# A fused attention and FFN block: every piece placed by a list schedule, and the loads in order of use

## The chip, the cores and the metric

One core of a Trainium2 chip. The time is the device time of one execution in microseconds. The span is the time from the first to the last instruction of a profiled or timed run; it is some 2 us shorter than the time. Every run also gives the mean clock that TensorE was granted (1.0 is full speed). Runs are compared within the same rounds on the same chip, and only fast runs are; a run over 1.5% above the fastest of the same kernel counts as slow.

## What the kernel computes

A layer norm of x (2048 rows, 640 columns, bf16) feeds two branches, whose sum with x is the output:

```python
def _A_ref(x, wqkv, wo):            # 32 heads of 20; window of 8 keys, 2 apart
    qkv = (x @ wqkv).reshape(B, S, 3, H, Dh) ...
    idx = pos[:, None] - (jnp.arange(8) * 2)[None, :]
    logits = jnp.einsum("bhsd,bhswd->bhsw", q, kg) * Dh ** -0.5   # masked where idx < 0
    o = jnp.einsum("bhsw,bhswd->bhsd", softmax(logits), vg)
    return o.reshape(B, S, D) @ wo

def _B_ref(x, w1, b1, w2, b2):      # 640 -> 1536 -> 640
    return gelu(x @ w1 + b1) @ w2 + b2

xn = _layernorm(x)
return x + _A_ref(xn, A_wqkv, A_wo) + _B_ref(xn, B_w1, B_b1, B_w2, B_b2)
```

## The kernel before

The rows are worked on in four chunks of 512. For each chunk VectorE multiplies q with eight shifted copies of k, TensorE sums the products by head (the "logits"), softmax follows across TensorE, ScalarE and VectorE, TensorE expands the weights back over the head's columns (the "expansions"), and VectorE multiplies them with v. Projections, FFN and output blocks are dense matmuls. Products of TensorE pass through four accumulators (`psA`), the logits have a buffer of two banks, and an output block a pair of its own:

```python
    psA = ctx.enter_context(tc.tile_pool(name="psA", bufs=4, space=bass.MemoryType.PSUM))
    psL = ctx.enter_context(tc.tile_pool(name="psL", bufs=1, space=bass.MemoryType.PSUM))
    psO = ctx.enter_context(tc.tile_pool(name="psO", bufs=1, space=bass.MemoryType.PSUM))
    # ... (cut)
    load_x(0)                                  # four transfers on SyncE's queue
    for s in range(3):                         # q, k and v columns of wqkv
        nc.scalar.dma_start(wqkv_sb[:, :, s * D : (s + 1) * D], wqkv_v[:, :, s * D : (s + 1) * D])
    nc.sync.dma_start(b1_rt[0:FT, :], B_b1.rearrange("(t p) -> t p", p=P))
    load_x(1)
    nc.sync.dma_start(w1_sb[:], B_w1.rearrange("(t p) n -> p t n", p=P))
    # ... (cut: b2, w2, wo on SyncE's queue)
```

An output block is 18 pairs of matmuls and one eviction of two copies:

```python
    def outs(n):
        # ... (cut)
        for bl in range(BPC):
            # ... (cut: x is loaded again, VectorE adds b2 to it)
            lo = psO.tile([P, CH], F32, tag="lo", name="lo")
            hi = psO.tile([P, CH], F32, tag="hi", name="hi")
            srcs = [(hT[:, ft, cs], w2_sb[:, ft, :]) for ft in range(FT)]
            srcs += [(ident[:], xb2[:])]
            srcs += [(oT[:, t, cs], wo2[:, t, :]) for t in range(KT)]
            # ... (cut: for each of srcs one matmul into lo, one into hi)
            nc.scalar.copy(osb[:, 0:CH], lo[:])
            nc.scalar.copy(osb[:, CH:D], hi[:, 0 : D - CH])
            nc.scalar.dma_start(out_sd[b * P : (b + 1) * P, :], osb[:])
```

The framework's scheduler orders the pieces, by the order in which the program names them and by what is ready:

```python
    ln(0)
    qkv(0)
    ln(1)
    for n in range(NCH):
        attention(n)
        ffn1(n)
        if n + 1 < NCH:
            qkv(n + 1)
        # ... (cut: load and layer norm of chunk n + 2)
        if n > 0:
            outs(n - 1)
    outs(NCH - 1)
```

## Time and profile before

| | before |
|---|---|
| median (lowest to highest) | 278.5 us (274.83 to 278.62), 3 runs |
| profiled run | 276.86 us, span 275.1, mean TensorE clock 0.969 |
| TensorE busy | 233.7 us, 85% of the span |
| VectorE, ScalarE busy | 173.0 us, 125.0 us |

The prediction below shows the busy slices, the chain and the timelines. Here is only the list of TensorE's waits by matmul group (engine, output tile, line; after the arrow what ended the wait; then us in total, times, longest; lines are cut at the dots):

```profile
PE lo L336 <- ACT osb L341: 4.9, 8, 0.6
PE L L215 <- DVE prod L210: 3.6, 3, 2.1
PE xps L263 <- ACT ax L270: 2.7, 6, 0.7
...
PE pps L193 <- DMA wqkv_sb<-in_A_wqkv_dram: 1.7, 1, 1.7
```

A reader is to see two things. Most waits belong to steps of the attention, and most of that time lies in the first chunk, the only one in which TensorE has no other work to put beside them. And `lo` waits for its own eviction eight times. The list counts only what the profile sees as idle and models the end of a matmul late, so it understates: from start to start of the matmuls the eight waits are 0.78 each.

### The profile page before, as it was taken

How to read it: one execution, taken by the hardware profiler on the slowest of the kernel's cores; microseconds unless marked ns; L12 is line 12 of the kernel's file. 1: busy time of each engine (PE TensorE's matmuls, PEld its weight loads, DVE VectorE, ACT ScalarE, POOL GpSimd, SP SyncE). 2: the span in 40 equal slices, each digit the busy share in tenths (PEclk: the TensorE clock that was granted, in tenths of full speed). 3: DMA queues.
4: the chain of work that ended last, by engine and by line, in shares of the span. 5: the costliest groups of instructions: out<-in, count | busy, mean ns of one | idle time of the engine just before them, and what ended most of it. 6: DMA issues, size and time to landing. Idle time of an engine off the chain costs nothing.

```text
span 275.1 us, 3746 instructions
## 1 busy us (share of the span) xinstructions
PE 233.7 (85%) x1564; PEld 122.4 (44%) x1591; DVE 173.0 (63%) x191; ACT 125.0 (45%) x212; POOL 0.9 (0%) x8
## 2 busy tenths in 40 slices
PE   0049995379999989999999989999999899999895
PEld 0024553124455543445555634455556444455452
DVE  3850599869965956997592259994932399921000
ACT  0242562576655546765551458655313586211211
POOL 1000000000000000000000000000000000000000
PEclk9999998559999999999999999999999999999999
DMA  7999203000000000000011110000021100111010
GB/s 249 373 335 381 92 2 95 24 4 0 0 0 2 0 26 24 0 2 0 0 49 49 50 49 0 2 0 0 10 88 50 48 0 0 50 48 48 26 48 24
DMA packets 11416, 15.47 MB, mean 56 GB/s; under 512 B 904, under 2 KB 10632, under 8 KB 11400
## 3 DMA queue, kind: packets, MB, share of 16 engines
q1 hardware_dynamic: 7128, 10.16, 11.3%
q10 hardware_dynamic: 4272, 5.08, 5.3%
q8 instruction: 12, 0.20, 0.3%
q14 instruction: 4, 0.03, 0.0%
HBM read 12.62 MB, written 2.62 MB: 55 GB/s over the span
## 4 chain that ended last, share of the span: by engine, by line
PE 71%; DVE 12%; ACT 7%; DMA 7%; issue 2%; SPq 0%; DVEq 0%; ACTq 0%
PE lo L336 20%; PE hps L307 19%; PE pps L193 18%; DVE prod L210 10%; PE hi L337 6%; DMA wqkv_sb<-in_A_wqkv_dram 4%; ACT osb L341 3%; PE xps L263 3%; DMA xc<-in_A_x_dram 3%; PE L L215 2%; ACT ax L270 1%; PE ssum L252 1%; ACT L249 1%; DVE m L238 1%; ACT e L249 1%
## 5 line engine op out<-in xcount | busy, mean ns | idle before, releaser
L193 PE MATMUL pps<-xnT,wqkv_sb 128*128 128x512 bf16 x296 | 68.0, 390 | 2.8 <-DMA wqkv_sb<-in_A_wqkv_dram 1.7
L336 PE MATMUL lo<-w_sb,hT 128*128 128x512 bf16 x177 | 52.4, 379 | 5.2 <-ACT osb L341 4.9
L210 DVE TENSOR_TENSOR prod<-qT,kvT 128x2560 bf16<-128x2560 bf16 x32 | 45.5, 1484 | 17.6 <-ACT kvT L200 17.6
L307 PE MATMUL hps<-xnT,w_sb 128*128 128x512 bf16 x235 | 54.0, 388 | 0.4 <-issue 0.2
L284 DVE TENSOR_TENSOR pv<-kvT,ax 128x2560 bf16<-128x2560 bf16 x32 | 45.5, 1484 | 10.4 <-ACT ax L270 10.4
L193 PEld LDWEIGHTS <-wqkv_sb 128*128 128x128 bf16 x300 | 35.6, 119 | 34.7 <-DMA wqkv_sb<-in_A_wqkv_dram 3.3
L337 PE MATMUL hi<-w_sb,hT 128*128 128x128 bf16 x192 | 42.2, 220 | 0.6
L314 ACT ACTIVATE hT<-hps,b1T 128x512 bf16<-128x512 f32 x48 | 32.6, 687 | 15.8 <-PE hps L307 15.4
L307 PEld LDWEIGHTS <-w_sb 128*128 128x128 bf16 x240 | 23.9, 100 | 30.1 <-issue 3.6
L341 ACT CAST osb<-lo 128x512 bf16<-128x512 f32 x16 | 9.4, 586 | 58.7 <-PE lo L336 53.7
L200 ACT CAST kvT<-pps 128x512 bf16<-128x512 f32 x40 | 23.4, 585 | 18.9 <-PE pps L193 18.9
L336 PEld LDWEIGHTS <-hT 128*128 128x128 bf16 x192 | 18.7, 98 | 24.2 <-issue 4.0
L327 DVE TENSOR_TENSOR xb<-xb,b2bc 128x640 bf16<-128x640 bf16 x16 | 7.8, 487 | 32.5 <-PE hi L337 32.5
L336 PE MATMUL lo<-wo,oT 128*128 128x512 bf16 x77 | 23.1, 379 | 0.0
L337 PEld LDWEIGHTS <-hT 128*128 128x128 bf16 x192 | 18.7, 97 | 9.5 <-issue 8.8
L293 DVE TENSOR_TENSOR pv<-pv 128x5120 bf16<-128x5120 bf16 x8 | 22.6, 2820 | 0.1
L270 ACT CAST ax<-xps 128x512 bf16<-128x512 f32 x32 | 16.1, 626 | 7.1 <-PE xps L263 7.1
L200 ACT CAST qT<-pps 128x512 bf16<-128x512 f32 x20 | 11.7, 585 | 15.0 <-PE pps L193 15.0
L337 PE MATMUL hi<-wo,oT 128*128 128x128 bf16 x80 | 17.5, 219 | 0.2
L147 DVE BATCH_NORM_STATS2 stats<-xc 128x6 f32<-128x320 bf16 x16 | 7.6, 477 | 14.7 <-DMA xc<-in_A_x_dram 14.7
L215 PE MATMUL L<-prod,head_of 128*32 128x256 bf16 x320 | 12.2, 283 | 3.7 <-DVE prod L210 3.6
L167 PE MATMUL tp<-ident,xn 128*128 128x128 bf16 x80 | 7.1, 243 | 7.1 <-DVE xn L157 7.0
(51 smaller groups left out, 148.4 us busy)
## 6 DMA issues: line engine op xcount, KB each, us to landing
w_sb<-in_B_w_dram SPq DMA_DIRECT2D x2, 1920.0 KB, 12.2
xc<-in_A_x_dram SPq DMA_DIRECT2D x16, 160.0 KB, 4.7
xb<-in_A_x_dram SPq DMA_DIRECT2D x16, 160.0 KB, 2.2
out_dram<-osb ACTq DMA_DIRECT2D x16, 160.0 KB, 1.8
wqkv_sb<-in_A_wqkv_dram ACTq DMA_DIRECT2D x3, 800.0 KB, 8.6
wo<-in_A_wo_dram SPq DMA_DIRECT2D x1, 800.0 KB, 17.0
b2bc<-in_B_b_dram SPq DMA_DIRECT2D x1, 160.0 KB
b_rt<-in_B_b_dram SPq DMA_DIRECT2D x1, 3.0 KB
```

The costliest lines, as they stand in the source:

```text
L193: nc.tensor.matmul(ps[:], lhsT=wv[:, ti, to, :], rhs=xnT[:, ti, :], start=(ti == 0), stop=(ti == KT - 1),)
L200: nc.scalar.copy(body[:, to, :], ps[:])
L210: nc.vector.tensor_tensor(out=prod[:, i, :, :], in0=qT[:], in1=kT[:, :, off : off + CH], op=ALU.mult)
L215: nc.tensor.matmul(L[j * H : (j + 1) * H, 2 * wp : 2 * wp + 2, :], lhsT=head_of[:], rhs=prod[:, :, t, j * P : (j + 1) * P], start=(t == 0 ...
L270: nc.scalar.copy(ax[:, 4 * g : 4 * g + 4, j * P : (j + 1) * P], xps[:].rearrange("p (w c) -> p w c", w=4))
L284: nc.vector.tensor_tensor(out=pv[:, i, :, :], in0=vT[:, :, off : off + CH], in1=ax[:, w, :].unsqueeze(1).to_broadcast([P, KT, CH]), op=ALU ...
L293: nc.vector.tensor_tensor(out=a[:], in0=a[:], in1=pv[:], op=ALU.add)
L307: nc.tensor.matmul(hps[:], lhsT=w1_sb[:, ti, ft * P : (ft + 1) * P], rhs=xnT[:, ti, :], start=(ti == 0), stop=(ti == KT - 1),)
L314: nc.scalar.activation(hT[:, ft, :], hps[:], ACT.Gelu_apprx_tanh, bias=b1T[:, ft : ft + 1], scale=1.0)
L336: nc.tensor.matmul(lo[:], lhsT=lhs, rhs=rhs[:, 0:CH], start=(k == 0), stop=(k == nk - 1))
L337: nc.tensor.matmul(hi[:, 0 : D - CH], lhsT=lhs, rhs=rhs[:, CH:D], start=(k == 0), stop=(k == nk - 1))
L341: nc.scalar.copy(osb[:, 0:CH], lo[:])
```

## The change

The intent is to keep TensorE in dense work from the first projection to the last output block. A small list scheduler in Python runs when the kernel is built: each piece (a projection group, a Gelu, a product, one of the five parts of an output block) has an engine, a length in us taken from earlier measurements, a rank, the pieces that it needs and the buffers that it holds. On each engine the ready piece of lowest rank starts first. The resulting order is issued and pinned on TensorE, VectorE and ScalarE: the framework may not reorder it there. With it go: all x resident (it is loaded once and b2 added in place), finer Gelu tiles (18 buffers), a third buffer for the transposed input, odd output blocks of the last chunk in the accumulators, a mask product of 64 columns instead of 512, outputs sent on SyncE's queue, and the loads in order of use.

```diff
-    load_x(0)
-    for s in range(3):
-        nc.scalar.dma_start(wqkv_sb[...], wqkv_v[...])
-    ... (cut: b1, x of chunk 1, w1, b2, w2, wo on SyncE's queue)
+    for bl in range(BPC):
+        (nc.sync, nc.scalar)[bl % 2].dma_start(x_sb[:, bl, :], x_nb[:, bl, :])
+    for s in range(3):
+        nc.sync.dma_start(wqkv_sb[...], wqkv_v[...])
+    nc.sync.dma_start(b1_rt[0:FT, :], B_b1.rearrange("(t p) -> t p", p=P))
+    ... (cut: x of chunks 1 to 3, w1, b2, w2, wo, all on SyncE's queue)
+def make_plan(fns):
+    ...
+        pl.add(f"ex{n}", SE, 2.4, n - 1000, [f"mx{n}"], f("exp", n), [L, e])
+        pl.add(f"rs{n}", SE, 0.3, -98, [f"st{n}{bl}" for bl in range(BPC)], f("sqrt", n, 0, BPC))   # n > 0
+        for ft in range(FT):
+            pl.add(f"f1{n}{ft}", PE, 1.08, base + 10 + ft, [f"tc{n}{bl}" for bl in range(BPC)], f("f1", n, ft), [xnT, ps], 21.0)
+            pl.add(f"ge{n}{ft}", SE, 0.6, base, [f"f1{n}{ft}"], f("ge", n, ft), [ps, hTs[ft]])
+    ... (cut: the other pieces in the same form)
-    for n in range(NCH):
-        attention(n)
-        ffn1(n)
-        ... (cut)
+    engines = {mybir.EngineType.PE, mybir.EngineType.DVE, mybir.EngineType.Activation}
+    with tc.manual_schedule(engines=engines):
+        for t in make_plan(fns).run():
+            t["fn"]()
```

The arguments of `add` are: name, engine, length, rank, needs, function, buffers, and an earliest time (for loads).

> **What bounds the kernel now.** I read the page's busy slices first, then the chain that ended last, then the timelines of TensorE and ScalarE.
>
> ```profile
> PE   0049995379999989999999989999999899999895
> DVE  3850599869965956997592259994932399921000
> PEclk9999998559999999999999999999999999999999
> GB/s 249 373 335 381 92 2 95 24 4 0 0 0 2 0 26 24 0 2 0 0 49 49 50 49 0 2 0 0 10 88 50 48 0 0 50 48 48 26 48 24
> ```
>
> Each digit is a slice of 6.9 us. TensorE (PE) is full from slice 9 to the end. It is nearly empty in slices 0 to 2 and thin in slices 6 to 8, and there its clock falls to half. VectorE (DVE) is never full for long: 173.0 us of 275.1. So TensorE is the bound, with two holes at the front. The chain shows the first:
>
> ```profile
> 2.10 7.14 DMA xc<-in_A_x_dram
> 9.27 11.39 DMA wqkv_sb<-in_A_wqkv_dram
> 20.70 8.45 PE pps L193 x27
> ```
>
> TensorE waits until 20.70 for the third piece of wqkv, which was issued only at 9.27 and took 11.39 us. The timeline of TensorE shows the second hole:
>
> ```profile
> 40.66 0.81 PE L167 MATMUL tp<-ident,xn 128*128 128x128 bf16 x10 [0.38 <-DVE xn L157]
> 41.40 1.05 PE L215 MATMUL L<-prod,head_of 128*32 128x256 bf16 x31
> 43.82 0.73 PE L215 MATMUL L<-prod,head_of 128*32 128x256 bf16 x20 [1.36 <-DVE prod L210]
> 46.62 1.25 PE L215 MATMUL L<-prod,head_of 128*32 128x256 bf16 x20 [2.07 <-DVE prod L210]
> ...
> 50.15 1.01 PE L240 MATMUL L<-m,negident 128*128 128x512 bf16 x2 [1.32 <-DVE m L238]
> 52.55 1.01 PE L252 MATMUL ssum<-e,ident 128*128 128x128 bf16 x8 [1.39 <-ACT e L249]
> 55.95 0.61 PE L263 MATMUL xps<-attn,rep 32*128 32x512 bf16 x4 [2.38 <-DVE attn L256]
> ```
>
> From 39.1 to 59.2 it serves only the attention of the first chunk: small matmuls between waits. The FFN of the same chunk, whose input has been ready since 18.3, starts after it. Later chunks have the previous chunk's output blocks to fill this hole, the first has none. Last, the ScalarE timeline near the end:
>
> ```profile
> 260.33 0.58 ACT L341 CAST osb<-lo 128x512 bf16<-128x512 f32 x1 [4.91 <-PE lo L336]
> ...
> 265.99 0.58 ACT L341 CAST osb<-lo 128x512 bf16<-128x512 f32 x1 [4.91 <-PE lo L336]
> ```
>
> One output block takes 5.66 us. It is 18 pairs (lo, hi), and a pair starts every 0.27 us in the dense parts: 4.86 us. The other 0.8 us is the eviction of the only lo/hi buffer.
>
> **What TensorE must do.** From starts in the timeline (busy times overlap, so I don't sum them): 300 projection and 240 FFN matmuls at 0.2156 us (five per 1.078 us, the distance of the evictions): 64.7 and 51.7. 16 output blocks: 77.8. 16 groups of 20 logit matmuls: 0.54 back to back, 0.8 between other work, say 12.8. Transposes of three chunks 3.6. Max subtraction 1.8, sums 1.9, 32 expansions at 0.1: 3.2. Sum 217.5 us. So of 275.1 some 57 is not TensorE work: 20.7 before the first dense matmul, 2.4 of slow first matmuls, 20.1 less 5.7 of work (80 logit matmuls, the transposes of a chunk, the mask, subtraction, sum and expansions) = 14.4 in the first attention, 2.0 for the FFN at half clock after it, 3.4 after the last matmul, and about 15 spread over evictions and waits in the later chunks.
>
> [...] the second and fourth gaps between q evictions are 2.13 and 1.08 us for five. [...] The trace has 1283 ns; [...] (a copy ends at 60.60, the load starts at 60.62). I count 1.3. [...]
>
> **The change part by part.**
> Loads: x of chunk 0 goes over both queues, then wqkv, b1, the rest of x, w1, b2, w2, wo on one queue. The order view shows that the second projection matmul still waits for all three pieces of wqkv. They need 0.65 + 2.46 = 3.1 MB; at the 335 to 381 GB/s of the slices and data from about 2 us on that is 10.5 to 11.5 us, not 20.7.
> Layernorm of chunk 0, by blocks: statistics from 3.3 at 0.87 a block. The Sqrt table load now waits for the first statistics (4.3), so the first rstd comes at 6.0; two more blocks and reciprocals to 8.15, first xn 8.6, the constants 0.85, the other xn to 10.9, transposes and copy 1.2: first projection at 12.2. This, not the load, is the later. Gain 8.5.
> First attention: the pinned order puts seven FFN groups, all of chunk 1's q and k projections and its transposes around the attention of chunk 0. By my count the hole shrinks to two: the order has Exp, then a Sqrt for chunk 3, which loads two tables (1.28 + 1.02 + 1.28 + 0.30) while three projections and the sum hold all four accumulators: about 1.4. Then eight expansions in a row paced by ScalarE at 0.50 each: about 2.6. So 4.0 in place of 14.4, and no half-clock stretch (2.0). Gain 12.4.
> Later chunks: FFN groups stand between most output blocks, so the eviction is hidden, and in the last chunk odd blocks use the accumulators. By the order three places keep an output block directly after another in the same buffer: 3 x 0.9 = 2.7. I add 2.7 for expansions and table loads that hold accumulators in chunks 1 to 3. So 5.4 in place of 15. Gain about 9.6.
> b2 is added once per chunk (4 instructions of about 1.5 against 16 of 0.49), x isn't loaded twice, output DMAs leave ScalarE (16 x 0.35): all off the bounding engine, worth nothing by themselves. ScalarE gets 11 table loads for 10.
> Sum: 12.2 + 2.4 + 217.5 + 4.0 + 5.4 + 3.4 = 244.9 us span, 30 less. The profiled run before had 276.86 us for a span of 275.1, and the median is 3.4 above it; I add 2: 247.
>
> I checked that VectorE doesn't become the bound. Attention costs it per chunk 8 x 1.425 (q by k) + 1.22 + 0.96 + 1.22 + 8 x 1.425 (v) + 3 x 2.82 + 1.49 = 36.2; four times that is 145, plus about 12 for the layernorms and b2 sums left after the start at 26.3: 183, well before TensorE ends. Following its order by hand, its last large sum is done near 208, and the last oT then waits for its buffer until the last block of chunk 2 is through (near 221), ahead of its use near 227.
>
> **The rivals.**
> A: the plan's lengths are wrong enough to make a chain of new waits. For: an exponential is planned with one table load, but the return to Gelu and the Sqrt of chunk 3 are planned without theirs, Gelu is planned at 0.6 and follows itself at 0.68, and logits between other work cost 0.8, not 0.6. Each engine is held in order, so one lateness is passed on. Against: most planned lengths match the profile (1.08, 0.52, 1.47, 2.82), and with 217 us on TensorE lateness elsewhere is mostly absorbed. It would give 252 to 258.
> B: the schedule is as good as it looks on paper, and the accumulator waits vanish in the four buffers: 12.2 + 2.4 + 217.5 + 3.4 + 2 for small waits + 2 = 239.5.
> C: one queue is slower than two, so that wqkv lands at 15 or later, and b2, for which VectorE waits in order ahead of the first q by k product, comes after 26. For: b2 stands behind 7 MB. Against: slice 3, when wqkv has landed and SyncE's queue works alone, has 381 GB/s. It would add 3 to 5.
> D: [...]the gain is only the start: 278 - 8.5 = 269. Against: the second hole is visible and fillable with ready work.
>
> **Range and chances.** The start and the first attention are solid: about 21 of the 30. The 9.6 of the later chunks may be half or may be more. So 247, with 239.5 (B) to 256 (most of A, or C) to hold 8 in 10. Even D is over 2% faster: faster 0.97, same 0.02, slower 0.01.
>
> **What would show it.** Right: the first projection near 12 (11 to 13); no half clock after the start; TensorE full from slice 3 on; a wait of 1 to 2 us of projections on ScalarE near 46 and the paced expansions after 50; the first q by k product near 26; the last matmul near 241. Wrong: projections that wait for wqkv beyond 13; repeated waits of TensorE for VectorE in chunks 2 and 3 (then A); outputs waiting for oT near the end; a half-clock stretch in the middle.

What is cut from the prediction, at the marked places, are statements of the hardware that don't come from this case's traces, among them the reason given why a pinned order has its gain and its risk, and the premise of rival D; neither is shown here. What is left between the marks are readings of the trace of before: the gaps between evictions of q, five matmuls each; the 1283 ns of one table load (all ten last as long); and the copy that ends just before the load of Gelu's table begins. No term of the sum is among the cuts: it is still 12.2 + 2.4 + 217.5 + 4.0 + 5.4 + 3.4 = 244.9, and 247 with the 2 for the time.

## The result

| | before | after |
|---|---|---|
| median (lowest to highest) | 278.56 us (274.83 to 278.77), 4 runs | 249.32 us (248.63 to 251.26), 4 runs |
| profiled span, mean clock | 275.1, 0.969 | 246.7, 1.0 |
| TensorE busy | 85% | 91% |

The ratio of the times is 0.899, with a 95% interval of 0.890 to 0.908. A ratio here is the mean time of one kernel's fast runs over that of the other's fast runs of the same rounds, so not quite the ratio of the medians. The change is faster by 10%.

The busy slices of the kernel after (tenths of busy time in 40 equal slices of 6.2 us):

```profile
PE   0489999889899999999979999999989999989994
PEclk9999999999999999999999999999999999999999
GB/s 235 365 378 378 269 0 3 1 0 0 3 0 0 3 0 19 11 0 29 0 27 29 0 0 0 29 0 29 0 28 3 27 27 28 2 27 27 29 53 27
```

TensorE is full from slice 3 on (counted from 0), and no slice has a lower clock. The loads run at 365 to 378 GB/s until nearly all are in, in the fifth slice.

The start of the chain that ended last (start, us, what):

```profile
0.73 2.94 DMA x_sb<-in_A_x_dram
4.92 1.28 ACT L353
...
11.29 1.96 ACT xnT L383 x3
13.30 7.77 PE pps L413 x29
```

The 11.39 us of wqkv are gone from the chain. In its place stands the layer norm: x lands, then come statistics, the table load of the square root (line 353), transposes and their copies. The projections begin at 13.30.

The timeline of TensorE through the attention of the first chunk, after:

```profile
43.06 0.59 PE L480 MATMUL L<-m,negident 128*128 128x512 bf16 x2
43.49 3.40 PE L413 MATMUL pps<-xnT,wqkv_sb 128*128 128x512 bf16 x14
46.73 0.61 PE L499 MATMUL ssum<-e,ident 128*128 128x128 bf16 x8
48.42 3.40 PE L413 MATMUL pps<-xnT,wqkv_sb 128*128 128x512 bf16 x15 [1.08 <-ACT qT L424]
51.75 0.39 PE L519 MATMUL xps<-attn,rep 32*128 32x512 bf16 x3
52.49 2.33 PE L519 MATMUL xps<-attn,rep 32*128 32x512 bf16 x5 [0.35 <-ACT kT L424]
```

Where before a wait stood in front of every softmax step, FFN groups and projections of chunk 1 now stand. What is left is one wait of projections at 48.42 and the expansions, which from 52.49 on are paced by ScalarE's copies (from start to start 0.49 us each). The wait at 48.42 is for a ScalarE copy, and the timeline of ScalarE shows why that is late:

```profile
43.97 1.28 ACT L492 ACT_TABLE_LOAD   x1
45.26 1.02 ACT L492 ACTIVATE e<-L 128x1024 bf16<-128x1024 f32 x1
46.30 1.28 ACT L353 ACT_TABLE_LOAD   x1
47.60 0.30 ACT L353 ACTIVATE std<-mv,eps_t 128x4 f32<-128x4 f32 x1
47.80 1.54 ACT L424 CAST qT<-pps 128x512 bf16<-128x512 f32 x3
```

The exponential and the square root of chunk 3 load two tables in a row, while three finished projections and the sum hold the four accumulators. A change of table costs 1.3 us here: the Gelu before it, from 43.26 on, ends at 43.95, the load begins at 43.97 and takes 1.28, and the exponential begins at 45.26; the next change has the same. In the list of TensorE's waits after, the evictions have become three:

```profile
PE lo L593 <- ACT osb L599: 2.0, 3, 0.7
```

Where the 28.4 us of span came from can be counted from the starts of TensorE's matmuls. I count a wait where a matmul starts over 0.25 us later than the dense distance of the one ahead of it allows (0.2156 us for 512 columns; for the smallest matmuls it is a choice, and a recount with 0.027 for a logit matmul and 0.1 for an expansion gives waits of 14.4 and 14.0 before, 4.6 and 5.0 after).

| us | before | after | gain |
|---|---|---|---|
| first dense projection | 20.7 | 13.3 | 7.4 |
| waits from there to 65 us | 15.0 | 4.7 | 10.3 |
| waits later | 12.5 | 4.5 | 8.0 |
| all else up to the last matmul | 223.3 | 220.6 | 2.7 |
| after the start of the last matmul | 3.6 | 3.7 | -0.1 |

"All else" is the matmuls themselves, with the half-rate ones. Before, the clock record has 17.1 us of half clock in the middle, from 46.2 to 63.2 (the FFN matmuls in it start 0.43 us apart, those behind it 0.216); after, none. Both kernels also run their first projections at half rate (0.43 from start to start), until 25.7 before and until 16.1 after: from the first dense projection that is 5.0 and 2.8 us, a loss of 2.5 and 1.4. So 1.1 of the 2.7 belongs to the start.

### The profile page after: what moved, and what is told of

It is laid out like the page before. It is cut to its first block, busy times and chain, and to the rows that moved or that the text cites. A ratio compares the mean times of both kernels' runs of the same rounds, so it can differ in the third digit from the quotient of the medians.

```text
span 246.7 us, 3683 instructions
## 1 busy us (share of the span) xinstructions
PE 225.2 (91%) x1562; PEld 118.9 (48%) x1591; DVE 171.8 (70%) x172; ACT 125.3 (51%) x216; POOL 1.4 (1%) x18
## 4 chain that ended last, share of the span: by engine, by line
PE 74%; issue 12%; ACT 9%; DVE 2%; DMA 1%; ACTq 0%
PE pps L413 26%; PE lo L593 18%; PE hps L561 17%; PE hi L594 5%; PE L L451 4%; ACT ax L529 2%; ACT L572 2%; PE xps L519 2%; PE tp L379 1%; ACT xnT L383 1%; DMA x_sb<-in_A_x_dram 1%; ACT L353 1%; ACT osb L599 1%; ACT hT L572 1%; PE ssum L499 1%
## 5 line engine op out<-in xcount | busy, mean ns | idle before, releaser
L561 PE MATMUL hps<-xnT,w_sb 128*128 128x512 bf16 x232 | 55.1, 380 | 1.1 <-ACT hT L572 0.6
L413 PEld LDWEIGHTS <-wqkv_sb 128*128 128x128 bf16 x300 | 35.1, 118 | 33.0 <-issue 5.3
L539 DVE TENSOR_TENSOR pv<-vT,ax 128x2560 bf16<-128x2560 bf16 x32 | 45.8, 1485 | 7.4 <-ACT ax L529 7.4
L439 DVE TENSOR_TENSOR prod<-qT,kT 128x2560 bf16<-128x2560 bf16 x32 | 45.3, 1483 | 0.0
L572 ACT ACTIVATE hT<-hps,b1T 128x512 bf16<-128x512 f32 x48 | 32.2, 690 | 13.8 <-PE hps L561 13.3
L561 PEld LDWEIGHTS <-w_sb 128*128 128x128 bf16 x240 | 22.4, 98 | 26.5 <-issue 2.2
L548 DVE TENSOR_TENSOR pv<-pv 128x5120 bf16<-128x5120 bf16 x12 | 33.9, 2824 | 0.4
L424 ACT CAST vT<-pps 128x512 bf16<-128x512 f32 x20 | 11.7, 586 | 11.6 <-PE pps L413 11.6
L554 DVE TENSOR_TENSOR oT<-pv 128x2560 bf16<-128x2560 bf16 x4 | 6.0, 1492 | 15.2 <-PE hi L594 15.1
L424 ACT CAST qT<-pps 128x512 bf16<-128x512 f32 x20 | 11.5, 585 | 9.6 <-PE pps L413 9.6
L424 ACT CAST kT<-pps 128x512 bf16<-128x512 f32 x20 | 11.8, 589 | 9.0 <-PE pps L413 9.0
L504 DVE RECIPROCAL rs<-ssum 128x128 f32<-128x128 f32 x4 | 3.8, 948 | 14.5 <-PE ssum L499 14.5
## 6 DMA issues: line engine op xcount, KB each, us to landing
x_sb<-in_A_x_dram SPq DMA_DIRECT2D x3, 640.0 KB, 10.3
```

The costliest lines, as they stand in the source:

```text
L413: nc.tensor.matmul(ps[:], lhsT=wqkv_p[:, ti, which, to, :], rhs=xnT[:, ti, :], start=(ti == 0), stop=(ti == KT - 1),)
L424: nc.scalar.copy(dest[:, to, off : off + CH], tiles["pps", n, which, to][:])
L439: nc.vector.tensor_tensor(out=prod[:, i, :, :], in0=qkv_tile(n, 0)[:], in1=qkv_tile(n, 1)[:, :, off : off + CH], op=ALU.mult,)
L539: nc.vector.tensor_tensor(out=pv[:, i, :, :], in0=qkv_tile(n, 2)[:, :, off : off + CH], in1=tiles["ax", n][:, w, :].unsqueeze(1).to_broadc ...
L548: nc.vector.tensor_tensor(out=ta[:], in0=ta[:], in1=tb[:], op=ALU.add)
L561: nc.tensor.matmul(ps[:], lhsT=w1_sb[:, ti, ft * P : (ft + 1) * P], rhs=tiles["xnT", n][:, ti, :], start=(ti == 0), stop=(ti == KT - 1),)
```

## The experiments

The theory is the prediction's: the gain is three separate things, the loads at the start, the dense work put into the first attention, and the evictions hidden later; pinning in itself does nothing. The rivals: the loads only move a wait; VectorE's attention work is the real bound at the front, so that filling TensorE gains little there; pinning, not the order, is what pays. I tried single parts on the kernel before (e1, e2), undid single parts of the kernel after (e3 to e6), and then measured the remaining waits (e7 to e10) and tried to remove them (e11, e12). All results but e7's are correct.

One thing has to be known for differences under 2 us: the runs of one kernel fall into groups by clock. The kernel after had spans of 246.7 and 247.2 at a mean clock of 1.0, 247.6 at 0.997 and 249.5 at 0.993. A clock of 0.993 means one stretch of 3.4 us at half clock in the profiled run of e7, which has it (from 54.70 to 58.10, right behind the expansions), and I take it to mean the same in the other runs. The kernel before does the same: spans of 272.9 to 275.3 at 0.968 to 0.974, and 275.3 to 277.0 at 0.956.

### e1: the kernel before, with the start of the loads as after

```diff
-            nc.sync.dma_start(xc[:, bl, :], ...)
+            q = nc.scalar if n == 0 and bl % 2 else nc.sync
+            q.dma_start(xc[:, bl, :], ...)
-        nc.scalar.dma_start(wqkv_sb[...], wqkv_v[...])
+        nc.sync.dma_start(wqkv_sb[...], wqkv_v[...])
-    nc.sync.dma_start(b1_rt[0:FT, :], ...)
+    nc.scalar.dma_start(b1_rt[0:FT, :], ...)
```

> The kernel before with only the start of the loads as in the changed kernel (x of chunk 0 on both queues, wqkv on the SyncE queue ahead of the rest; b1 on the ScalarE queue, since this kernel's first transpose waits for it). Theory, that the gain at the start is the arrival of wqkv and everything after it shifts: the second projection matmul starts near 13.3 us instead of 20.7, and the time falls by about 7 us, ratio to before 0.975. Rival, that the early start is eaten by the first attention or by w1, which the FFN needs: the first projection is as early, but the time falls by less than 2 us.

Measured: 272.03 us (271.38 to 273.19), ratio 0.985 (0.979 to 0.991; unclear against a bound of 2%), span 5.5 shorter. The timeline of TensorE, and the clock row of the busy slices:

```profile
11.65 18.78 PE L194 MATMUL pps<-xnT,wqkv_sb 128*128 128x512 bf16 x75 [0.84 <-ACT xnT L169]
```

```profile
PEclk9999975599999999999999999999999689999999
```

The first projection comes at 11.65 instead of 20.70, 9 us earlier. The first attention ends 8.7 earlier too (50.51 instead of 59.20), with the same hole in it. But the time gained only 4 and the span 5.5. The clock row says where some of it went: besides the 17 us in the hole there is a second half-clock stretch of 6.8 us at 211 to 218, and all four runs have the mean clock (0.954 or 0.955) that goes with it. Were that stretch full of matmuls it would cost 3.4, which with 5.5 is 8.9. The two traces settle where the rest went: output matmul for output matmul, e1 is 8.65 us ahead of before up to its own 210.9, and 5.48 ahead from 229.0 to the end. All 3.17 are lost across this stretch. So the load order is worth nearly 9 us where it acts; why the stretch came in all four runs of e1 isn't shown.

Why the third piece of wqkv was late before is in the trace: its issue at 9.27 waits on the semaphore of the fourth x transfer, which landed at 9.25 (the two were given the same one). In e1 and after, wqkv is among the first transfers and its issue (2.66, 2.68) waits for nothing.

### e2: the kernel before, with the FFN of chunk 0 named ahead of its attention

```diff
+    ffn1(0)
     for n in range(NCH):
         attention(n)
-        ffn1(n)
+        if n > 0:
+            ffn1(n)
```

> The kernel before with only the FFN of chunk 0 emitted ahead of its attention. Theory, that the hole in the first attention (14.4 us and 2.0 of half clock) is for want of work that is ready: 60 matmuls (12.95 us) and some output work move into it, and the time falls by 8 to 11 us, ratio 0.96 to 0.97. Rival, that placing the block in front only moves the hole behind it, since the softmax chain of about 11 us after the last product remains without filler: the time falls by less than 4 us.

Measured: 269.67 us (269.65 to 270.20; a fourth run in the slow state is left out), ratio 0.977 (0.969 to 0.985; unclear against a bound of 2%), span 7.2 shorter. The timeline of TensorE:

```profile
39.94 13.35 PE L307 MATMUL hps<-xnT,w_sb 128*128 128x512 bf16 x60
...
62.79 0.40 PE L263 MATMUL xps<-attn,rep 32*128 32x512 bf16 x4 [2.38 <-DVE attn L256]
```

The FFN moved into the hole whole, and the rival that filling gains less than 4 fell. It was a little under what was expected: the expansions still wait, for VectorE and then for ScalarE (5.1 in all from 62.79 on), and new waits of 2.8 and 1.1 stand at 87 to 89. Two half-clock stretches of 3.4 us remain (from 65.05 and from 88.94). Of the 7.2 us some 1.4 are not the edit's: in this run wqkv landed at 19.48 and not at 20.65, and the projections are 1.4 ahead before the FFN begins. Three lines of program order, without any scheduler, are worth a fifth to a quarter of the change.

### e3: the kernel after, with the loads as before

```diff
-        (nc.sync, nc.scalar)[bl % 2].dma_start(x_sb[:, bl, :], ...)
+        nc.sync.dma_start(x_sb[:, bl, :], ...)
-        nc.sync.dma_start(wqkv_sb[...], wqkv_v[...])
+        nc.scalar.dma_start(wqkv_sb[...], wqkv_v[...])
     ... (cut: x of later chunks block by block, in the old places)
```

> The changed kernel with the old queues: wqkv on the ScalarE queue, x of chunk 0 on the SyncE queue, then b1, x of chunk 1, w1, b2, w2, wo, and the rest of x last. Theory: the projections start near 20 us instead of 13.3, TensorE cannot make it up because it is full afterwards, so the span is 6 to 8 us longer than 246.7 and the ratio to before about 0.92 to 0.93. Rival, that the schedule has slack to absorb it: less than 3 us longer.

Measured: 256.69 us (254.90 to 257.54), ratio 0.928 (0.922 to 0.934), span 253.0, clock 1.0. The timeline of TensorE:

```profile
19.50 5.86 PE L414 MATMUL pps<-xnT,wqkv_sb 128*128 128x512 bf16 x19 [1.53 <-DMA wqkv_sb<-in_A_wqkv_dram]
```

Dense projections begin at 19.50 instead of 13.30: 6.2 later, and the span is 6.3 longer. In a kernel that is dense from then on, the start goes into the end one for one.

### e4: the kernel after, with other dense work held until the first attention is over

```diff
+    hold = [f"xc0{g}{j}" for g in range(2) for j in range(BPC)]   # the copies of chunk 0's expansions
-  pl.add(f"pj{n}{which}{to}", ..., [f"tc{n}{bl}" for bl in range(BPC)], ...)
+  pl.add(f"pj{n}{which}{to}", ..., [f"tc{n}{bl}" for bl in range(BPC)] + hold * (n > 0), ...)
-  pl.add(f"f1{n}{ft}", ..., [f"tc{n}{bl}" for bl in range(BPC)], ...)
+  pl.add(f"f1{n}{ft}", ..., [f"tc{n}{bl}" for bl in range(BPC)] + hold, ...)
```

> The changed kernel with every FFN group and every projection of chunks 1 to 3 held in the plan until the expansions of chunk 0 are through (the rest is ordered by the same scheduler). Theory, that filling the first attention is worth the hole: idle TensorE there grows from 4.6 to 14 to 17 us, half clock comes back there for some us, and the span is 10 to 13 us longer than 246.7, ratio 0.93 to 0.945. Rival, that the list schedule finds the time again later, because it has more ready work then: less than 4 us longer.

Measured: 263.86 us (263.17 to 264.40), ratio 0.955 (0.950 to 0.960), span 261.8, 15.1 longer. The timeline of TensorE, and the clock row:

```profile
50.01 0.61 PE L520 MATMUL xps<-attn,rep 32*128 32x512 bf16 x4 [4.08 <-DVE attn L510]
...
54.30 8.73 PE L562 MATMUL hps<-xnT,w_sb 128*128 128x512 bf16 x30
```

```profile
PEclk9999995659999999999999999999999999999999
```

The kinds of wait that before had are back. All waits from the first projection on sum to 18.7, against 9.1 after: 9.6 more. The other 5.6 us are slower matmuls, in 17 us of half clock (38.0 to 44.9 and 48.3 to 58.5): of these, 2.2 can be read off at 54.30, where 30 FFN matmuls take 8.73 and 30 at 0.2156 would be 6.5; the rest I put down to the matmuls between the waits. I had expected 10 to 13. The hole costs its waits and, on top, the half clock that comes with it and reaches into the dense work behind it.

### e5: the kernel after, with the output blocks of a chunk one behind the other in one buffer

```diff
-  pl.add(f"f1{n}{ft}", ..., [f"tc{n}{bl}" for bl in range(BPC)], ...)
+  pl.add(f"f1{n}{ft}", ..., [f"tc{n}{bl}" for bl in range(BPC)] + [f"o{n-1}34"] * (n > 0 and ft > 5), ...)
-            own = n < NCH - 1 or bl % 2 == 0
+            own = True
     ... (cut: the same in the plan's buffers; outputs wait for FFN group 5 of the next chunk)
```

> The changed kernel with the second half of each FFN held until the four output blocks of the chunk before are done, and with no accumulators used for the odd blocks of the last chunk. By its order a block then follows another directly in the same buffer seven times instead of three. Theory: each such place costs 0.83 us, so four more waits of 0.83 show and the span is 3 to 4 us longer than 246.7. Rival, that evictions do not set the time: within 1 us of it.

Measured: 252.29 us (252.01 to 254.44), ratio 0.913 (0.906 to 0.921), span 3.6 longer. The list of TensorE's waits:

```profile
PE lo L593 <- ACT osb L599: 4.6, 7, 0.7
```

Seven eviction waits instead of three. From start to start each is 0.83, so four more are 3.3 of the 3.6.

### e6: the kernel after, issued in the same order but not pinned

```diff
-    with tc.manual_schedule(engines=engines):
-        for t in make_plan(fns).run():
-            t["fn"]()
+    for t in make_plan(fns).run():
+        t["fn"]()
```

> The changed kernel with the same pieces issued in the same order, but without pinning, so that the framework's own scheduler may reorder. The order view shows that it hoists a few output matmuls of chunk 0 into the first attention and between the expansions, and keeps the rest of the start. Theory, that the order is what gains and the pinning is not needed: within 1.5% of the changed kernel, ratio to before 0.89 to 0.912. Rival, that the pinning is what gains: above 0.93.

Measured: 251.57 us (250.69 to 251.92), ratio 0.908 (0.901 to 0.916), span 3.0 longer, clock 1.0. The timeline of TensorE:

```profile
13.75 12.76 PE L413 MATMUL pps<-xnT,wqkv_sb 128*128 128x512 bf16 x48 [1.60 <-DMA wqkv_sb<-in_A_wqkv_dram]
```

Left to itself, the framework keeps most of the order, but not all. It moves the late square root ahead of the exponential and output matmuls into the softmax, so that the wait of after at 48.42 is gone (the projections at 50.30 follow the sum at once). In exchange it waits 1.97 at 13.75 for wqkv and 1.56 at 96.66 for VectorE. At under 1% from after, pinning isn't what pays; the order is.

### e7: the kernel after without the square root of chunk 3 (wrong on purpose)

```diff
+        if n == 3:
+            nc.scalar.copy(std[:, sl], mv[:, sl, 1])
+            return
```

The variance stands in for its root, so the last chunk is wrong, and one table load is gone.

> The changed kernel with the Sqrt of chunk 3, which stands between the first Exp and the copies of the projections, replaced by a plain copy (the result for chunk 3 is wrong on purpose); the order on each engine stays. It takes away one table load of 1.28 us. Theory: the wait of 1.24 us of TensorE for the copy of q at 48.4 goes, and the span falls by 1.0 to 1.3 us. Rival, that TensorE then waits as long for the Exp or for accumulators held by something else: the span stays within 0.4 us.

Measured: 249.70 us (248.83 to 249.84), ratio 0.902 (0.895 to 0.908), span 247.8. The timeline of TensorE:

```profile
47.45 0.61 PE L502 MATMUL ssum<-e,ident 128*128 128x128 bf16 x8
47.90 3.40 PE L416 MATMUL pps<-xnT,wqkv_sb 128*128 128x512 bf16 x15
```

The wait is gone: the projections follow the sum at once. So the table load was its cause. That its 1.24 us are worth 1.24 us of time isn't shown. The profiled run had a half-clock stretch right behind the expansions (first and second column: the window and its length; last but two: the clock):

```profile
50.00:54.70 4.70, 3.76 (x17) 1.23 (x15) 1.10 (x2) 3.95 (x9) 0.00 (x0) 1.00 0.00 0
54.70:58.10 3.40, 3.18 (x9) 1.21 (x9) 3.40 (x3) 1.73 (x4) 0.00 (x0) 0.50 0.00 0
```

Three of its four runs have the clock of 0.993 that goes with such a stretch, against one of four for after. In the one run at clock 1.0 the span is 246.7, as after. Matmul for matmul, e7 is 0.7 behind after ahead of the wait (the sum at 47.45 for 46.73), 0.5 ahead of it at the expansions (51.23 for 51.75), and 1.2 behind from the half-clock stretch on. So the 1.2 us are gained where the load was, and this run loses 1.7 in the stretch. In time it is inconclusive.

### e8, e9, e10: which of the two sets the start

e8 gives wqkv three tiles, so that the q projections need not wait for v's piece. e9 loads the table of the square root on a dummy value at the very start and does the constants behind the layer norm. e10 does both.

```diff
+    wqkv_t = [wts.tile([P, KT, D], BF16, name=f"wqkv{s}") for s in range(3)]     # e8, e10
-                lhsT=wqkv_p[:, ti, which, to, :],
+                lhsT=wqkv_p[which][:, ti, to, :],
+    nc.scalar.activation(warm[:], eps_t[:], ACT.Sqrt, bias=eps_t[:], scale=1.0)  # e9, e10
-        if n == 0 and b1 == BPC:
-            constants()
+        if n == 1 and bl == 0:
+            constants()
```

> The changed kernel with wqkv in three tiles, so that the q projections wait for the first 0.82 MB only (landed at 8.6) and not for all three (13.15). Theory, that the layernorm chain of chunk 0 (last copy at 13.24) holds the start as long as the load does: no gain, the first projection still near 13.3, span within 0.5 us of 246.7. Rival, that the load alone holds it: the first projection 1 us or more earlier.

> The changed kernel with a shorter layernorm chain for chunk 0: the Sqrt table is loaded ahead of the statistics and the constants are built after the four xn. Theory, that load and chain hold the start jointly: the transposed copy is done about 1.2 us earlier, but the second projection matmul still waits for wqkv until 13.15, and the span stays within 0.4 us of 246.7. Rival, that the chain alone held it: dense projections from 12.1 and 1 us less.

> Both changes to the start, three wqkv tiles and the shorter layernorm chain. Theory: now the start moves, dense projections from about 12.1, the span 1.0 to 1.3 us below 246.7. Rival, that something else (the clock of TensorE, x landing later, b2) takes it back: within 0.4 us.

Measured: e8 250.47 us (249.19 to 250.63), ratio 0.904 (0.897 to 0.911), first projection at 13.04. e9 251.32 us (248.28 to 251.78), ratio 0.908 (0.902 to 0.914), and the timeline of TensorE:

```profile
11.61 0.58 PE L415 MATMUL pps<-xnT,wqkv_sb 128*128 128x512 bf16 x1 [0.84 <-ACT xnT L385]
13.03 12.17 PE L415 MATMUL pps<-xnT,wqkv_sb 128*128 128x512 bf16 x48 [0.83 <-DMA wqkv_sb<-in_A_wqkv_dram]
```

e10 248.63 us (247.18 to 249.30), ratio 0.897 (0.892 to 0.902), with dense projections from 11.55.

Neither alone starts dense work earlier by more than 0.3 us; both together do, by 1.75. Two limits stood at the same place after: the layer norm's last copy ended at 13.24, and the third piece of wqkv landed at 13.15. The gain in span of e10's profiled run was only 0.7, since its first matmuls ran at half rate for longer: its first two evictions are 2.1 us apart and after's 1.4; the 50 matmuls from 11.55 took 12.9 us, after they took 12.2. In time e10 and after overlap, so the worth of the earlier start is not settled by these runs alone.

### e11: e10, and a plan told what was measured

The scheduler now keeps track of the table that ScalarE holds and adds 1.29 us for each change; the exponential goes down to 1.04; landing times, logits (0.7) and the first projection are as measured.

```diff
+                        need = {"rs": "sqrt", "ex": "exp", "ge": "gelu"}.get(best["name"][:2]) if eng == SE else None
+                        if need and need != table:
+                            us, table = us + 1.29, need
-        pl.add(f"ex{n}", SE, 2.4, ...)
+        pl.add(f"ex{n}", SE, 1.04, ...)
     ... (cut: landing times and lengths; e10's edits)
```

> Both changes to the start, and the plan told what the profile showed: a table load of 1.29 us whenever ScalarE changes function, logits of 0.7, slow first matmuls, and the landing times. Theory, that the plan's wrong lengths cost about 1.2 us in the first attention and little elsewhere: the span 2 to 3 us below 246.7. Rival, that a more exact plan gives nothing, since most of what is left are waits that the plan foresaw (expansions, evictions): the same as with the two changes to the start alone.

Measured: 246.41 us (246.32 to 246.69), ratio 0.890 (0.885 to 0.895), span 2.4 shorter than after. The timeline of ScalarE:

```profile
43.62 1.02 ACT L498 ACTIVATE e<-L 128x1024 bf16<-128x1024 f32 x1
44.54 1.56 ACT L430 CAST qT<-pps 128x512 bf16<-128x512 f32 x3
46.12 1.28 ACT L359 ACT_TABLE_LOAD   x1
```

The plan now puts three projection copies ahead of the square root, and TensorE's wait there is gone, in a correct kernel. This came although all four runs have a half-clock stretch (clock 0.991; 3.4 us from 52.09 in the profiled one). The three eviction waits of 0.83 remain, as does the pacing of the expansions.

### e12: the waits and some of the work taken away

On e11: four of the eight expansions are copied by VectorE; five late output blocks go into the two banks of the logits; from chunk 1 on VectorE evicts the outputs and adds x + b2 on the way, so that 12 identity pairs need no TensorE.

```diff
+LATE = ((1, 3), (2, 1), (2, 3), (3, 1), (3, 3))
-                pl.add(f"xc{n}{g}{j}", SE, 0.54, ...)
+                pl.add(f"xc{n}{g}{j}", VE if j % 2 else SE, 0.54, ...)
-            pl.add(f"oc{n}{bl}", SE, 0.78, ...)
+            pl.add(f"oc{n}{bl}", SE if n < 1 else VE, 0.78, ...)
-            if pc == 3:
+            if pc == 3 and n < 1:
                 srcs.append((ident[:], x_sb[:, n * BPC + bl, :]))
+        if n >= 1:      # eviction
+            nc.vector.tensor_tensor(out=osb[...], in0=tiles[part, n, bl][...], in1=x_sb[...], op=ALU.add)
     ... (cut: the buffers)
```

> All of that, and work taken off TensorE and its waits: late output blocks use the two banks of the logits as a second buffer; from chunk 1 on VectorE evicts the outputs and adds x and b2 there, so 12 identity pairs of 0.27 us are gone (3.2 us); VectorE makes half of the expansion copies. Theory, that TensorE's work and its waits are the time: 1.2 at the start, 1.2 for the table, two of three eviction waits (1.7), most of 2.6 at the expansions, 3.2 of work, so 8 to 10 us below 246.7: a span of 237 to 239 and a ratio of 0.86 to 0.87. Rival, that VectorE, which is full between 100 and 165 us, becomes late with evictions and copies and TensorE waits for it: 243 or more.

Measured: 238.71 us (238.15 to 239.70, six runs), ratio to before 0.862 (0.858 to 0.866), span 236.5, clock 1.0. The first part of the page:

```profile
PE 219.7 (93%) x1538; PEld 116.9 (49%) x1567; DVE 191.3 (81%) x212; ACT 108.3 (46%) x177; POOL 1.4 (1%) x18
```

One eviction wait is left (0.83, at 119.03). This kernel beats both others; against before it is 14% faster. Of the 10.2 us of span below after, 1.8 are the earlier start (11.50), 3.6 are waits (5.5 left of 9.1), and 3.2 by estimate are the 12 pairs at the 0.27 us of the prediction. The remaining 1.6 I did not trace. VectorE rose from 171.8 to 191.3 us and had the room.

## Why the prediction was right, and where it was off

The time came to 249.32 where 247 was predicted. By the steps of the sum:

- **The start.** 13.30 measured for 12.2. The layer norm was later: x landed from 3.68 on and the first table load began at 4.92. The first projections were slow for 1.4 and not 2.4, so the two together hit by luck (14.7 for 14.6). Wrong was the landing of wqkv: 13.15, where 10.5 to 11.5 had been worked out from bytes over bandwidth (its own figures give 10.2 to 11.3). The slices show 365 to 378 GB/s, so bandwidth was as assumed, but by 13.15 some 4.0 MB had moved by estimate (the first two slices and 0.8 us of the third, from the row of GB/s), not the 3.1 of x and wqkv: some of the later transfers was already coming in beside it. In e1 the figure came true: there the third piece landed at 11.43, with 3.5 MB moved. Behind wqkv on the queue e1 has x of chunk 1 in four transfers of 160 KB and b1 on the other queue; after has b1 and then x in transfers of 640 KB, and in the ten runs with these loads the piece landed between 12.89 and 13.96. Which of the two differences does it, no run separates. The late landing did no harm only because the layer norm ended at the same moment, which e9 shows: with a shorter layer norm the wait is for wqkv.
- **TensorE's work.** 219.2 for 217.5 (220.6 less the 1.4).
- **First attention.** Of the 4.0, the wait for two tables was 1.24 for 1.4, at 48.42 and not 46; the expansions cost 2.65 for 2.6. One wait that I had put with the later ones came at 63.28 (0.76, the return to Gelu's table). e7 and e11 show the cause of the first. No half clock appeared in the middle of the profiled run. By its clock of 0.993 one of the other three had the stretch of 3.4 us, the sign that the prediction had named against itself. It doesn't explain why the median is 0.7 above the profiled run: the two runs in the middle have clocks of 1.0 and 0.997.
- **Later chunks.** 5.2 with that one, for 5.4. The three evictions came where the order said, at 0.83 each for 0.9. e5 shows their price.
- **Tail.** 3.7 for 3.4; the last matmul started at 243.0 for 241.

The sum was 244.9 and the span 246.7. The parts in e3, e4 and e5 undo 6.3, 15.1 and 3.6 us, 25.0 of the 28.4; what they share or leave is 3.4. The smaller parts (x resident, b2 in place, the narrow mask, outputs on SyncE's queue) weren't undone singly.

In the prediction's comparison with before, two gains were taken too large. The start gave 7.4 and not 8.5 (the shorter half-rate beginning, not foreseen, gave the other 1.1), the later chunks 8.0 and not 9.6. The first attention gave more than its waits: 10.3 of waits, and most likely a good part of the 1.6 that remain of "all else", since e4 shows 5.6 us of slower matmuls when the hole is put back. What brings the half clock on isn't shown. The rates are (2.13 and 1.08 us for five matmuls), and the lengths of the stretches: 3.4 in e7, 6.8 in e1, 6.9 and 10.2 in e4, 17.07 in before. The waits of TensorE around them differ: in the hole of before they go up to 2.7 us; in e7 the stretch from 54.70 follows eight expansions, before which the timeline shows no idle time over 0.35. The same kernel has a stretch in some runs and not in others (e7: spans 247.5 to 247.8 at a clock of 0.993, 246.7 at 1.0). A slip of reading: the gap of 2.13 between q evictions is the first, not the second.

Of the rivals, A (a chain of new waits) showed only in the two table loads that it named; B counted 2 us of waits where 9.1 are left; C was half right, as wqkv was later than computed, but it gave no wait, and the first product of q and k started at 26.94 for 26.3; D fell with e4. The last oT came at 223.69 (predicted about 221), off the path.

## What to carry to other kernels

Find the engine that bounds the kernel, count its work from the distances of its starts, and account for the rest of the span as a list of waits; each can then be predicted, and undone, by itself. Ready work of another stage put into a hole is worth the hole and the half clock behind it (9.6 us of waits and 5.6 of slower matmuls in e4), and much of that is to be had by reordering the program; pinning an order needs a plan that knows the table loads (1.28 us each here), the landing times and which buffers are held. When two limits end at the same moment, removing one shows nothing: try both before dropping the idea.
